# Gates turned in 32x32 blocks on VectorE before they are stored to DRAM, in an attention kernel on one core

## The chip, the core and the metric

The kernel runs on one core of a Trainium2 chip. The metric is the device time of one execution in microseconds (us). Before the change it is 2564.84 us, the median of three runs (2561.96 to 2568.30 us). One more execution was profiled; its trace is what all views below come from.

## The reference, cut to what matters

```python
def _A_ref(x, wqkv, wo):                       # B the same, with its own weights
    B, S, D = x.shape;  H = 32;  Dh = D // H   # S 2048, D 512, Dh 16
    qkv = (x @ wqkv).reshape(B, S, 3, H, Dh).transpose(2, 0, 3, 1, 4)
    q, k, v = qkv[0], qkv[1], qkv[2]
    scores = jnp.einsum("bhqd,bhkd->bhqk", q, k) * (Dh ** -0.5)
    o = jnp.einsum("bhqk,bhkd->bhqd", _softmax(scores), v)
    return o.transpose(0, 2, 1, 3).reshape(B, S, D) @ wo

g = _sigmoid((x * gate_w).sum(-1, keepdims=True))
return g * _A_ref(x, A_wqkv, A_wo) + (1 - g) * _B_ref(x, B_wqkv, B_wo)
```

Two attention blocks of 32 heads each read the same x of 2048 tokens. A gate g per token mixes their outputs. The gate is small: 2048 numbers g and 2048 numbers 1 - g, 16 KB in all.

## The kernel before, in words

**Heads and half heads.** The 64 heads (32 of A, then 32 of B) run one after another through the same pipeline. A head's 2048 queries are taken in two halves. For a half, TensorE multiplies the 16 tiles of 128 keys with the 1024 queries (`score`, L305), ScalarE takes the exponential out of PSUM (L307), and TensorE multiplies the result with v into the accumulator `acc` (L974). Each half ends with a copy of `acc` to a tile `ev` (L997) and its store to the DRAM tensor `od` (L1002).

**The maxima, one half ahead.** The exponential needs the largest score of each query beforehand. TensorE therefore computes the scores of a later half a first time (L234), VectorE takes their maxima (L240, L252), and `max_split` and `max_rows` bring them to the place where the second computation uses them. That trip is made once for each half head, 128 times in all: VectorE turns the tile `mparts` of maxima into `mt` in 32x32 blocks (L270); SP stores `mt` into the DRAM tensor `md` in runs of 32 half-precision numbers, 64 bytes (L273); when that has landed, SP loads two rows of `md` into the rows 48 and 49 of `q_st` (L278, two loads); and the score matmuls of the half contract over 50 rows, these two among them (L305).

**What sets the order.** The order of every engine's instructions is fixed when the program is built. The string `FULL` spells out four rows of 128 queries at a time: letters for score tiles, maxima, products with v and hidden projection pieces. Two lists are emptied along it. `row_ops` holds what has a fixed place: one entry at each letter W or R, with `max_split` and `max_rows` put at its front at every half head. `waiting` holds DMA issues of SP without a fixed place; `drip(1)` pops one of them after every second score tile (L1054). So how many entries stand in `waiting` decides between which other issues of SP each one falls. SP itself works strictly in order: an issue that waits for a semaphore holds up all that stand behind it.

**The gates.** From row 26 + 8*16 on, the gate logits are summed (L560) and `queue_gates` puts nine steps into `row_ops`: eight of arithmetic on [128 x 16] tiles and `spread_gates`. `gate[0]` (g) and `gate[1]` (1 - g) hold token 128*t + p in partition p, column t. `spread_gates` puts 16 DMA issues into `waiting`. The first eight store `gate[s]` into the DRAM tensor `gd[s]`, in the token order that the heads use (issued at L108 through `drip`, and listed under L108 for that reason): each covers 64 partitions and 8 columns, and neighbouring tokens lie in neighbouring partitions, so that no two numbers of one partition are neighbours in DRAM. The other eight load runs of 128 tokens from `gd` into `gate_t` (L580), where all eight heads of a group get a copy. `gate_t` is read at L643, from 681.8 us on; `gate[1]` is read once more at the end (L776).

## Time and profile before

| what | value |
|---|---|
| time, median of 3 runs | 2564.84 us (2561.96 to 2568.30) |
| time of the profiled execution | 2568.01 us |
| its span, first to last instruction | 2566.2 us |
| what lies around the span | 1.8 us |
| mean granted TensorE clock | 0.997 |
| busy: TensorE, VectorE, ScalarE, GpSimd | 98%, 92%, 93%, 17% |
| gate stores (8) issued | 496.7 to 516.6 us |
| gate loads (8) issued | 517.2 to 524.9 us |
| first use of the loaded gates | 681.8 us |

TensorE is nearly never idle: what delays it is lost, since no later slack exists to make up for it. The views name instructions by line, engine, operation and tile: "q_st<-md" is the transfer from `md` into `q_st`. "SPq" stands for the issue of a DMA by SP; its duration is that of the issue, not that of the transfer. "PEld" is TensorE's loading of weights.

### The profile page before, as it was taken

The page shows a single profiled execution, that of the slowest core. Times are in us where ns is not written, and L with a number is a line of the kernel's source. Part 1 is how long each engine was busy: PE and PEld are TensorE (multiplying, and loading weights), DVE is VectorE, ACT ScalarE, POOL GpSimd, SP SyncE. Part 2 cuts the span into 40 slices and gives each one's busy share as a digit, 9 for nine tenths or more (in the row PEclk, how much of TensorE's full clock was granted, in tenths as well). Part 3 has the DMA queues.
Part 4 walks back from the last instruction along what each step waited for, and adds up shares of the span by engine and source line. Part 5 has one row for each costly group of instructions (what it writes and reads, how often), then busy time and mean ns, then how long its engine had stood idle before and what let it go on. Part 6 is the DMA issues. An engine that isn't in the chain of part 4 may idle for free.

```text
span 2566.2 us, 169681 instructions
## 1 busy us (share of the span) xinstructions
PE 2509.2 (98%) x76566; PEld 1608.9 (63%) x76566; DVE 2363.4 (92%) x4587; ACT 2399.0 (93%) x4750; POOL 434.3 (17%) x841
## 2 busy tenths in 40 slices
PE   9999999889999999999999999999999999999997
PEld 4666666556666666666666666655665566665663
DVE  4999999879999999999999999999999999999994
ACT  1899999889999999999999999999999999999995
POOL 3133211211210000111212112112101200002113
PEclk9999999989999999999999999999999999999999
DMA  6533223222211322322222222245113321124103
GB/s 144 149 87 87 69 67 99 51 70 68 79 52 53 84 57 55 102 67 78 70 59 68 68 82 56 67 127 136 41 49 95 90 58 49 36 78 113 46 21 117
DMA packets 150911, 195.24 MB, mean 76 GB/s; under 512 B 45368, under 2 KB 95816, under 8 KB 150184
## 3 DMA queue, kind: packets, MB, share of 16 engines
q1 hardware_dynamic: 144008, 172.45, 24.4%
q8 instruction: 599, 9.81, 1.7%
q0 software_dynamic: 3136, 9.74, 1.4%
q10 hardware_dynamic: 3040, 2.20, 0.3%
q14 instruction: 128, 1.05, 0.1%
HBM read 116.80 MB, written 66.59 MB: 71 GB/s over the span
## 4 chain that ended last, share of the span: by engine, by line
PE 85%; ACT 4%; DVE 4%; DMA 3%; issue 2%; SPq 1%; POOL 1%; ACTq 0%; POOLq 0%; DVEq 0%
PE acc L974 40%; PE ps_m L234 16%; PE ps_st L305 14%; PE ps_p L324 6%; ACT p L307 3%; PE ps_st L234 3%; DVE mxp L240 2%; PE ps_p L705 2%; PE ps_p L346 1%; DVE ev L997 1%; ACT ev L997 1%; PE ps_st L346 1%; DMA q_st<-md 0%; SPq L108 0%; DMA k_st<-early 0%
## 5 line engine op out<-in xcount | busy, mean ns | idle before, releaser
L974 PE MATMUL acc<-p,vg 64*17 64x384 f32 (+1 forms) x34784 | 2186.9, 365 | 18.9 <-issue 7.8
L307 ACT ACTIVATE p<-ps_st 128x512 f32<-128x512 f32 x4068 | 2122.4, 642 | 72.0 <-PE ps_st L305 30.6
L240 DVE TENSOR_REDUCE mxp<-ps_m 128x1 f32<-128x512 f32 x3072 | 1944.2, 683 | 77.8 <-PE ps_m L234 40.4
L305 PE MATMUL ps_st<-q_st,k_st 50*32 50x512 f16 x16272 | 1561.3, 381 | 17.5 <-DMA q_st<-md 13.7
L234 PE MATMUL ps_m<-k_st,q_st 48*32 48x512 f16 x14336 | 1380.3, 377 | 5.5 <-issue 4.0
L974 PEld LDWEIGHTS acc<-p,vg 64*17 64x17 f32 x34784 | 979.8, 93 | 249.0 <-issue 27.2
L305 PEld LDWEIGHTS <-k_st 50*32 50x32 f16 x16384 | 670.5, 90 | 387.8 <-issue 199.6
L234 PEld LDWEIGHTS <-q_st 48*32 48x32 f16 x16384 | 550.3, 90 | 232.6 <-issue 143.3
L324 PE MATMUL ps_p<-x_sb,w 64*32 64x512 f32 x3648 | 477.9, 591 | 0.2 <-issue 0.2
L252 DVE CUSTOM_DVE_ANT_0 rise<-ps_m,rise 128x512 f32<-128x512 f32 x512 | 350.0, 684 | 49.9 <-PE ps_st L305 38.5
L247 ACT ACTIVATE rise<-ps_st 128x512 f32<-128x512 f32 x512 | 316.8, 619 | 35.3 <-PE ps_st L234 23.3
L234 PE MATMUL ps_st<-x_st,q_st 48*32 48x512 f16 x2048 | 225.6, 377 | 1.2 <-DMA x_st<-rise_p 1.2
L264 POOL TENSOR_SCALAR mrow<-mrow 128x8 f32<-128x8 f32 x128 | 29.8, 233 | 1059.9 <-DVE mrow L263 1059.4
L371 POOL CAST parts<-stage 128x512 f16<-128x512 f32 x56 | 34.1, 610 | 809.0 <-ACT stage L832 438.1
L705 PE MATMUL ps_p<-w_big,ot 64*32 64x512 f32 x1024 | 134.4, 591 | 0.0
L324 PE MATMUL ps_p<-w_big,x_sb 64*32 64x512 f32 x1024 | 133.8, 590 | 0.0
L324 PEld LDWEIGHTS ps_p<-x_sb,w 64*32 64x32 f32 x3648 | 116.5, 106 | 18.7 <-issue 5.1
L705 PE MATMUL ps_p<-wo_b,ot 64*32 64x512 f32 x768 | 100.6, 591 | 1.9 <-ACT added L917 1.5
L346 PE MATMUL ps_p<-w_big,x_sb 64*32 64x256 f32 x1280 | 86.4, 376 | 0.0
L372 POOL TENSOR_TENSOR parts<-stage,parts 128x512 f16<-128x512 f32 x56 | 65.3, 1165 | 4.5
L346 PEld LDWEIGHTS ps_p<-w_big,x_sb 64*32 64x32 f32 x1280 | 42.2, 106 | 13.0 <-issue 1.4
L997 DVE COPY ev<-acc 128x512 f32<-128x512 f32 x64 | 44.2, 690 | 1.2 <-PE ps_p L324 0.4
(115 smaller groups left out, 836.2 us busy)
## 6 DMA issues: line engine op xcount, KB each, us to landing
od<-ev SPq DMA_DIRECT2D x126, 256.0 KB
k_st<-kd SPq DMA_DIRECT2D x126, 128.0 KB
q_st<-qd SPq DMA_DIRECT2D x126, 128.0 KB
vd<-v_st SPq DMA_DIRECT2D x64, 136.0 KB
vg<-vd POOLq DMA_DIRECT2D x32, 272.0 KB, 4.0
k_st<-kd SPq DMA_DIRECT2D x126, 64.0 KB
q_st<-qd SPq DMA_DIRECT2D x126, 64.0 KB
kd<-parts SPq DMA_DIRECT2D x56, 128.0 KB
```

The lines of the kernel that those rows point to most:

```text
L234: pe.matmul(ps[j:j + 32], q[b:b + SC, t * P + j:t * P + j + 32], k[b:b + SC], start=True, stop=True, tile_position=(b, j))
L240: dve.tensor_reduce(o[:, c:c + 1], ps, op=ALU.max, axis=AX.X)
L247: act.activation(rises[m], ps, AF.Relu)
L252: dve.tensor_tensor_reduce(out=rise, in0=ps, in1=rise, scale=1.0, scalar=LOWEST, op0=ALU.add, op1=ALU.max, accum_out=o[:, 0:1])
L305: pe.matmul(ps[j:j + 32], k[b:b + SC + 2, kk * P + j:kk * P + j + 32], qv(b), start=True, stop=True, tile_position=(b, j))
L307: act.activation(pt[u][:, c * 512:(c + 1) * 512], ps, AF.Exp, scale=SCALE / UNIT ** 2)
L324: pe.matmul(ps[j:j + 32], a, m, start=k == 0, stop=k == last, tile_position=(b, j))
L346: pe.matmul(ps[j:j + 32, e * 256:(e + 1) * 256], x_sb[b:b + 64, i, k, o:o + 32], w_big[b:b + 64, k, g * P:(g + 2) * P], start=k == e == 0, ...
L372: pool.tensor_tensor(t[:n, 1], v[:n], t[:n, 0], op=ALU.subtract)
L705: pe.matmul(ps[j:j + 32], T["o"][b:b + 64, k, o + j % 64:o + j % 64 + 32], w[b:b + 64, g], start=first, stop=last, tile_position=(b, j))
L974: pe.matmul(acc[d:d + 17, qa * P:qb * P], v[b:b + 64, 2 * (w % n) + c if h == NH - 1 else w % n, j], pt[u][b:b + 64, c * 512 + qa * P:c * ...
L997: (dve.tensor_copy if w < NT or h == NH - 2 else act.copy)(ev, acc)
```

## The change

The two gate tiles become the two halves of one tile [128 x 2 x 16], and the two DRAM tensors one tensor [2, 2048]. VectorE turns the [128 x 32] tile in 32x32 blocks into a new tile `gate_r`: there a partition 32*a + 16*s + t holds the 32 tokens 128*t + 32*a to 128*t + 32*a + 31, so that one partition's 32 numbers are 128 neighbouring bytes in DRAM. Four stores, one for each a, take the place of eight. The eight loads into `gate_t` read the same order of tokens as before.

```diff
-    gd = [dram.tile([S], F32, name=f"gd{s}") for s in range(2)]
+    gd = dram.tile([2, S], F32, name="gd")
...
-    gate = [core.tile([P, NT], F32, name=f"gate{i}") for i in range(2)]
+    gates = core.tile([P, 2, NT], F32, name="gate")
+    gate = [gates[:, i] for i in range(2)]
...
     def spread_gates():
+        turned = core.tile([P, 32], F32, name="gate_r")
+        dve.transpose(turned, gates.rearrange("p s t -> p (s t)"))
+
+        def store_part(a):
+            nc.sync.dma_start(bass.AP(tensor=gd.tensor, offset=gd.offset + a // 2 * 512 + a % 2 * 32,
+                                      ap=[[1024, 4], [64, NT // 2], [1, 32]]), turned[32 * a:32 * a + 32])
+
         def one(s, i, f):
-            o = gd[s]
             nc.sync.dma_start(gate_t[s][f * 64 + i * 32:f * 64 + i * 32 + 32], bass.AP(
-                tensor=o.tensor, offset=o.offset + i * 1024 + f * 512, ap=[[0, HG], [P, 4], [1, P]]))
-
-        for s in range(2):
-            o = gd[s]
-            for i in range(2):
-                for f in range(2):
-                    waiting.append((nc.sync.dma_start, bass.AP(
-                        tensor=o.tensor, offset=o.offset + i * 1024 + f * 512, ap=[[1, 64], [64, NT // 2]]),
-                        gate[s][f * 64:f * 64 + 64, i * NT // 2:(i + 1) * NT // 2]))
+                tensor=gd.tensor, offset=gd.offset + s * S + i * 1024 + f * 512, ap=[[0, HG], [P, 4], [1, P]]))
+
+        waiting.extend((store_part, a) for a in range(4))
         waiting.extend((one, s, i, f) for s in range(2) for i in range(2) for f in range(2))
```

Four entries fewer in `waiting` move the issues of SP against each other. This is SP's order before, from the last projection store ahead of the gates; `kd`, `xd` and `qd` take projections, and `w` is the next group's weights:

```order
L366 DMA xd_97<-rise_p 64x2x512
L108 DMA gd_116<-gate_1604 64x8x1 x4
L108 DMA gd_117<-gate_1605 64x8x1 x2
L273 DMA md_115<-mt 4x32x32
L278 DMA q_st_231<-md_115 2x1024 x2
L108 DMA gd_117<-gate_1605 64x8x1 x2
L580 DMA gate_t_1611<-gd_116 32x1x128 x4
L580 DMA gate_t_1612<-gd_117 32x1x128 x4
L1002 DMA od_106<-ev 128x512
L360 DMA qd_81<-parts 64x2x512 x2
L118 DMA w_15244<-in_wqkv_a 64x4x128 x4
```

Six gate stores stand ahead of the store of the maxima (`md`), and no gate load. The same place now, each row with the semaphores that it waits for (DMAHW0 to DMAHW7 count the transfers of SP in turn; each transfer takes the next one):

```order
L366 DMA xd_97<-rise_p 64x2x512 [waits DMAHW4_49,Pool_49]
L583 DMA gd<-gate_r 4x8x32 [waits DMAHW5_49]
L583 DMA gd<-gate_r 4x8x32 [waits DMAHW6_49]
L583 DMA gd<-gate_r 4x8x32 [waits DMAHW7_49]
L583 DMA gd<-gate_r 4x8x32 [waits DMAHW0_49]
L587 DMA gate_t_1609<-gd 32x1x128 [waits DMAHW6_49,DMAHW5_49,DMAHW1_49]
L587 DMA gate_t_1609<-gd 32x1x128 [waits DMAHW7_49,DMAHW2_49,DMAHW0_49]
L273 DMA md_115<-mt 4x32x32 [waits DMAHW3_49,DVE_49]
L278 DMA q_st_230<-md_115 2x1024 [waits DMAHW4_49,DMAHW3_49]
L278 DMA q_st_230<-md_115 2x1024
L587 DMA gate_t_1609<-gd 32x1x128 x2
L118 DMA w_15085<-in_wqkv_a 64x4x128 [waits DMAHW4_49,PE_49]
```

All four gate stores and the first two gate loads now stand ahead of the store of the maxima, and these two loads wait for the gate stores (DMAHW5, 6, 7 and 0). The weight load has moved ahead of the store of `ev`. On VectorE one row is added, behind the two gate steps and half a head ahead of those stores:

```order
L240 TENSOR_REDUCE mxp<-ps_m 128x1 x2
L572 TENSOR_TENSOR gate<-gate_u,gate_e 128x16
L1072 TENSOR_SCALAR gate<-gate 128x16
L580 STREAM_TRANSPOSE gate_r<-gate 128x32
L252 ISA rise,mxp<-ps_m,rise 128x512
```

Here L580 is a line of the changed kernel: the blockwise turn of the gates. The orders of TensorE, ScalarE and GpSimd are the same as before.

## Prediction

> **What bounds the kernel now.** I read the page first, for the engine that sets the time; then stretches of the trace cut at equal places of the program, for where it loses; then the waits, SP's own timeline and VectorE's in the worst stretch.

> ```profile
> PE 2509.2 (98%) x76566; PEld 1608.9 (63%) x76566; DVE 2363.4 (92%) x4587; ACT 2399.0 (93%) x4750; POOL 434.3 (17%) x841
> PE   9999999889999999999999999999999999999997
> PEclk9999999989999999999999999999999999999999
> ```

> TensorE is busy 98% of the span. In 40 slices of 64 us only the eighth and ninth (449 to 577 us) fall under nine tenths before the end, and in the ninth the granted clock falls too. The gate stores are issued in just these slices. The turn of the maxima (L270) comes once in each half head, so stretches from one turn to the next hold equal work:

> ```profile
> core 0: us, PE busy (x) PEld busy (x) DVE busy (x) ACT busy (x) POOL busy (x), PEclk, DMA share, GB/s
> 478.97:498.28 19.31, 19.17 (x600) 12.89 (x602) 18.55 (x39) 18.87 (x38) 5.41 (x8) 1.00 0.28 71
> 498.28:537.59 39.31, 23.09 (x600) 13.53 (x602) 18.72 (x37) 19.47 (x38) 2.47 (x6) 0.83 0.17 30
> 537.59:556.53 18.94, 18.89 (x600) 12.56 (x602) 18.27 (x37) 18.66 (x38) 3.23 (x6) 1.00 0.37 102
> 556.53:575.46 18.93, 18.85 (x600) 12.61 (x601) 18.23 (x36) 18.65 (x38) 3.96 (x8) 1.00 0.27 74
> ```

> Each has 600 matmuls. One takes 39.31 us where the next two take 18.94 and 18.93: 20.4 us are lost. TensorE's idle time there is 39.31 - 23.09 = 16.2 us against 0.1 in the next ones; the other 4.2 us (23.09 against 18.89) are matmuls at a lower granted clock, 0.83 on the mean. What ends the idle time:

> ```profile
> PE ps_st L305 <- DMA q_st<-md: 11.5, 1, 11.5
> 503.98 0.41 PE L234 MATMUL ps_m<-k_st,q_st 48*32 48x512 f16 x3 [1.59 <-issue]
> 509.61 0.45 PE L974 MATMUL acc<-p,vg 64*17 64x256 f32 x3 [2.76 <-issue]
> ```

> The longest wait, 11.5 us, is for the rows of maxima. Two more, 1.6 and 2.8 us, have no releaser in the trace; they fall into the same time. SP shows why the maxima are late:

> ```profile
> 496.06 0.57 SPq L366 DMA_DIRECT2D xd<-rise_p  x1
> 496.69 9.00 SPq L108 DMA_DIRECT2D gd<-gate  x6
> 505.78 1.46 SPq L273 DMA_DIRECT2D md<-mt  x1
> 515.35 0.53 SPq L278 DMA_DIRECT2D q_st<-md  x2
> 515.93 1.27 SPq L108 DMA_DIRECT2D gd<-gate  x2
> 517.24 8.25 SPq L580 DMA_DIRECT2D gate_t<-gd  x8
> ...
> 479.20 0.58 SPq L273 DMA_DIRECT2D md<-mt  x1
> 481.18 0.53 SPq L278 DMA_DIRECT2D q_st<-md  x2
> ```

> The last two rows are the same trip one half head earlier. There `md` is issued 0.23 us after the turn, and its landing lets the load go 481.18 - 479.20 = 1.98 us after that. In the bad stretch the six gate stores hold SP for 9.0 us, so that `md` goes 505.78 - 498.28 = 7.5 us after the turn; it then takes 9.57 us (to 515.35), and TensorE starts again only at 522.74, 11.53 us after it stopped at 511.21. The traffic of the time is small in bytes and large in number:

> ```profile
> DMA packets 4201, 0.22 MB, mean 10 GB/s; under 512 B 4058, under 2 KB 4194, under 8 KB 4198
> gd<-gate SPq DMA_DIRECT2D x8, 2.0 KB
> md<-mt SPq DMA_DIRECT2D x1, 8.0 KB
> 522.74 0.62 PE L305 MATMUL ps_st<-q_st,k_st 50*32 50x512 f16 x4 [11.53 <-DMA q_st<-md]
> ```

> The first row is for 496.5 to 518 us: 4201 packets for 0.22 MB. A gate store of 2 KB in runs of 4 bytes is 512 pieces, the eight are 4096; `md` is 8 KB in 128 runs of 64 bytes. So I read the loss as one cause, 4096 single-element writes, with three effects: SP held, the maxima's two transfers slow, and other waits of TensorE in the same time.

> **The change part by part.**

> *The single elements go.* 4096 pieces of 4 bytes become 4 x 32 = 128 runs of 128 bytes, the count that `md` has in every half head, where it costs 1.98 us to its landing and no idle time of note. If the stretch falls to the length of its neighbours, the gain is 39.31 - 18.94 = 20.4 us; against the stretch before it (19.31, with the gate arithmetic on GpSimd and VectorE in it) it is 20.0 us. I take -20.4 us, then subtract what the new order costs.

> *The turn on VectorE.* It comes behind the two last gate steps:

> ```profile
> 478.97 0.20 DVE L270 STREAM_TRANSPOSE mt<-mparts 128x32 f16<-128x32 f16 x1
> 480.58 0.17 DVE L1071 TENSOR_SCALAR gate<-gate 128x16 f32<-128x16 f32 x1
> 480.86 0.69 DVE L252 CUSTOM_DVE_ANT_0 rise<-ps_m,rise 128x512 f32<-128x512 f32 x1
> 498.28 0.20 DVE L270 STREAM_TRANSPOSE mt<-mparts 128x32 f16<-128x32 f16 x1
> ```

> The nearest row is the turn of `mparts`, the same 128x32 at half the bytes: 0.20 us. With 32-bit numbers I bound it by 0.2 and 0.4 us and take 0.2. It delays the maximum at 480.86. VectorE is busy 18.55 of 19.31 us in that stretch, so 0.76 us of slack stand against it: 0 to 0.4 us, taken as 0.1. Its result is ready 16 us before the first store needs it.

> *The wait that stands ahead of the maxima now.* SP issues four stores and two gate loads before `md`, and the second load waits until the last two stores have landed. Queued behind that wait are `md`, the two `q_st` loads that TensorE needs, six more gate loads, the weight load and the store of `ev`. The clock of it: SP is free at 496.69, after `xd`. Below are, in this order, two gate stores of the chain of waits before SP was held (issue 0.63 us, a step of 0.68 from one to the next), SP's timeline in two other half heads, TensorE's wait in the first of these, and both as stretches from turn to turn:

> ```profile
> 499.54 0.63 SPq L108
> 500.22 0.64 SPq L108
> ...
> 1658.95 3.90 SPq L140 DMA_DIRECT2D wo_b<-in_wo_b  x5
> 1662.94 0.58 SPq L273 DMA_DIRECT2D md<-mt  x1
> 1665.32 0.99 SPq L278 DMA_DIRECT2D q_st<-md  x2
> 1280.71 0.58 SPq L273 DMA_DIRECT2D md<-mt  x1
> 1283.02 0.53 SPq L278 DMA_DIRECT2D q_st<-md  x2
> PE ps_st L305 <- DMA q_st<-md: 1.7, 1, 1.7
> 1278.47:1297.45 18.98, 18.90 (x600) 12.41 (x602) 18.25 (x37) 18.74 (x38) 2.46 (x6) 1.00 0.27 76
> 1659.47:1679.16 19.69, 17.61 (x508) 9.15 (x501) 18.07 (x40) 18.32 (x39) 1.14 (x5) 1.00 0.57 162
> ```

> The fourth store is issued at 496.69 + 3 x 0.68 = 498.7 and has landed, priced like `md`, 1.98 us later at 500.7. The first load has gone before that; the second goes at 500.7 and takes 0.65 to 1.03 us (8.25 / 8). So `md` goes at about 501.4 instead of 498.5, the `q_st` loads at 503.4 to 503.8 (1.98 to 2.38 us, the latter from 1662.94 to 1665.32, where other issues are close by), and SP has issued both by 504.3 at the latest: 5.6 to 6.0 us after the turn at 498.28. How late is too late, these two half heads tell, where loads of weights stood ahead of the maxima. With the loads issued by 1283.02 + 0.53, 5.1 us after the turn at 1278.47, the half head takes 18.98 us: nothing lost. With 1665.32 + 0.99, 6.8 us after the turn at 1659.47 (five loads of `wo_b` stood ahead), TensorE waits 1.7 us and the half head takes 19.69, 0.75 us more than 18.94. Between these, 5.6 to 6.0 us cost 0.2 to 0.4 us. A landing of 3.6 us in place of 2, because gate loads run beside it, would make it 1 to 2 us. I take 0.5 us, with 0 and 2 as ends. The granted clock in the row of 1659.47 is 1.00, so a wait of this size doesn't slow the matmuls behind it.

> *What else moves.* The weight load now comes before the store of `ev`. Its tile was last read for the projections whose results `xd` stores at 496.06, so I cost it at nothing; were the tile still in use, the store of `ev` would wait behind it, and two `ev` buffers cover that for one half head. `gate_t` is used at 681.8 us: at nothing.

> The sum: -20.4 + 0.5 + 0.1 = -19.8 us. Against the profiled execution that is 2568.01 - 19.8 = 2548.2 us (its span 2566.2 - 19.8 = 2546.4, with the same 1.8 us around it). The profiled execution stands 3.2 us above the median; taking the same difference off the median gives 2564.84 - 19.8 = **2545.0 us**.

> **The rivals.**

> *A wait takes the place of the one removed (10%).* The 128-byte stores might land as late as `md` did in the bad stretch, 9.57 us after issue instead of 1.98. Then the second gate load goes at 498.7 + 9.57 = 508.3, `md` at 508.9, the `q_st` loads are issued by 511.5, 13.2 us after the turn. That is 6.4 us beyond the case of 1659.47, where TensorE waited 1.7, so it waits 8.1 us; with the loss to the clock in the proportion of the bad stretch (20.4 lost for 16.2 idle), 10.2 us. Gain 10.2, time 2554.6. Against it: `md` itself has runs half as long, as many of them, and lands in 1.98 us. [...]

> *Slower: the stores still go out by single elements (3%).* Should a partition's 32 numbers be cut into 4-byte pieces, four stores of 1024 pieces stand ahead of the maxima in place of six of 512, and SP also waits for their landing. At 9.00 / 6 = 1.5 us for 512 pieces they hold SP 12 us, to 508.7; the last lands 9.57 us after its issue at 505.7, at 515.3; gate load, `md` and its landing (2 to 9.6 us) and the loads end at 519 to 526, and with the 6.9 us that followed in the bad stretch (515.88 to 522.74) TensorE starts at 526 to 533 instead of 522.74. That is 3 to 10 us slower: 2568 to 2575. It decides as soon as the stores need over some 20 us from first issue to landing. Against it: the run is contiguous on both sides, in a partition of `gate_r` and in DRAM.

> *No gain: without the profiler the stall isn't there (4%).* Then the times of the unprofiled runs would lack it already, and the change moves nothing: 2564.8. Against it: unprofiled runs would have to be 20 us under the profiled one; the median is 3.2 under, the fastest (2561.96) 6.1. This bounds what the stall costs without the profiler to 14 us at the least, and is why I let the range reach up.

> **How the numbers follow.** The forecast has 83%, with a range of its own of 2542 to 2552: 2545.0, down by the 0.6 us of added cost and the spread of the runs (2.9 below the median), up by 2 us for the wait and 5 for a smaller stall outside the profile. The first rival has 10%, no gain 4%, slower 3%. What a measurement of this kernel can tell from no change is some 0.3%, 7.7 us. Forecast and first rival both lie beyond that; of the forecast's weight I move 1% to "same" for a smaller stall. So faster 0.92, same 0.06 (no gain, that 1%, and the part of the slower case under 7.7 us), slower 0.02. A range of 2541 to 2556 takes in the forecast and the first rival and leaves out under a tenth by the cases; my unknown is the size outside the profile.

> **What would show it.** Right: the stretch of 39.31 us becomes one of 19 to 20 with 600 matmuls at a granted clock of 1.00; the four gate stores take about 2.7 us of SP; `md` follows the turn by about 3 us and its landing takes about 2; the wait for the maxima is under 2 us; packets under 512 bytes fall by some 3970 of the 45368 of the page. The unnamed waits of 1.6 and 2.8 us have to vanish too: if they stay, they had another cause. Wrong: `md` landing after 5 us or more (first rival), gate stores holding SP for several us each (slower), or a new long wait elsewhere that takes the 20 us back.

## The result, and the profile after

| | before | changed |
|---|---|---|
| time, median | 2563.40 us (4 runs, 2560.11 to 2568.30) | 2545.81 us (4 runs, 2545.46 to 2549.03) |
| ratio | | 0.9933, 95% interval 0.9914 to 0.9951 |
| profiled execution, its span | 2568.01, 2566.2 us | 2545.46, 2543.7 us |
| half head in which the gates are stored | 39.31 us | 19.03 us |

The change makes the kernel faster by 0.67% (0.49% to 0.86%), 17.2 us of 2563.4. The forecast was 2545.0 us. The kernel before has one more run here than ahead of the prediction, hence 2563.40 in place of 2564.84. The profiled execution of the changed kernel is one of its four runs.

The first lines of the page of the changed kernel are the busy time of each engine, then TensorE and its granted clock in 40 slices, then the DMA packets of the whole span:

```profile
PE 2503.8 (98%) x76566; PEld 1610.5 (63%) x76566; DVE 2363.4 (93%) x4588; ACT 2396.5 (94%) x4750; POOL 433.4 (17%) x841
PE   8999999999999999999999999999999999999997
PEclk9999999999999999999999999999999999999999
DMA packets 146831, 195.24 MB, mean 77 GB/s; under 512 B 41288, under 2 KB 91736, under 8 KB 146104
```

The dent in the eighth and ninth slices is gone, and with it the dip of the clock. Packets under 512 bytes fell from 45368 to 41288, by 4080 where some 3970 were forecast; the new stores account for 3968 (4096 less 128), what the other 112 were, no view shows. The stretches from one turn of the maxima to the next, with the gate stores in the middle one, as before (span, then busy time of each engine, granted clock, DMA share, GB/s):

```profile
480.15:499.15 19.00, 18.89 (x599) 12.51 (x601) 18.62 (x39) 18.72 (x38) 5.39 (x8) 1.00 0.29 73
499.15:518.18 19.03, 18.95 (x602) 12.51 (x607) 18.24 (x36) 18.69 (x38) 2.46 (x6) 1.00 0.28 82
518.18:537.07 18.89, 18.84 (x599) 12.52 (x597) 18.22 (x37) 18.64 (x37) 3.22 (x6) 1.00 0.30 81
```

39.31 us became 19.03, as good as its neighbours. SP's timeline in the changed kernel around the gates:

```profile
496.93 0.57 SPq L366 DMA_DIRECT2D xd<-rise_p  x1
497.55 2.60 SPq L583 DMA_DIRECT2D gd<-gate_r  x4
500.27 1.70 SPq L587 DMA_DIRECT2D gate_t<-gd  x2
502.06 0.57 SPq L273 DMA_DIRECT2D md<-mt  x1
504.04 0.53 SPq L278 DMA_DIRECT2D q_st<-md  x2
```

Four stores take 2.60 us, the two gate loads with their wait 1.70, and the maxima go at 502.06, 2.91 us after their turn; 1.98 us later they have landed and are loaded. What TensorE still waits for them, among the waits of 499 to 519 us, and the two turns on VectorE:

```profile
PEld L305 <- DMA q_st<-md: 0.4, 1, 0.4
```

```profile
481.97 0.21 DVE L580 STREAM_TRANSPOSE gate_r<-gate 128x32 f32<-128x32 f32 x1
499.15 0.20 DVE L270 STREAM_TRANSPOSE mt<-mparts 128x32 f16<-128x32 f16 x1
```

The profiled executions differ by 22.5 us, 20.3 of them in this stretch. The rest lies where the change does nothing: the half head that took 21.23 us at 1789.8 in the trace before takes 18.93 in the trace after, and a start that is 2.4 us longer after (64.29 against 61.91 us to the first turn) is made up in other places. Differences of this kind stand between other traces too: the half head right ahead of the one with the gate stores takes 18.94 to 19.31 us in the thirteen traces of this case.

### The profile page after: what moved, and what is told of

It reads as the page before. It is cut to its first block, busy times and chain, and to the rows that moved or that the text cites. A ratio compares the mean times of both kernels' runs of the same rounds, so it can differ in the third digit from the quotient of the medians.

```text
span 2543.7 us, 169678 instructions
## 1 busy us (share of the span) xinstructions
PE 2503.8 (98%) x76566; PEld 1610.5 (63%) x76566; DVE 2363.4 (93%) x4588; ACT 2396.5 (94%) x4750; POOL 433.4 (17%) x841
## 2 busy tenths in 40 slices
DMA packets 146831, 195.24 MB, mean 77 GB/s; under 512 B 41288, under 2 KB 91736, under 8 KB 146104
## 4 chain that ended last, share of the span: by engine, by line
PE 85%; ACT 5%; DVE 4%; DMA 2%; issue 2%; SPq 0%; POOL 0%; ACTq 0%; POOLq 0%; DVEq 0%
PE acc L975 40%; PE ps_m L234 16%; PE ps_st L305 14%; PE ps_p L324 6%; ACT p L307 3%; PE ps_st L234 3%; DVE mxp L240 3%; PE ps_p L706 2%; PE ps_p L346 1%; DVE ev L998 1%; ACT ev L998 1%; PE ps_st L346 1%; DMA md<-mt 0%; PE ps_m L324 0%; DMA w<-in_wqkv_a 0%
## 5 line engine op out<-in xcount | busy, mean ns | idle before, releaser
L305 PE MATMUL ps_st<-q_st,k_st 50*32 50x512 f16 x16272 | 1558.4, 380 | 7.4 <-ACT p L307 2.4
L234 PE MATMUL ps_m<-k_st,q_st 48*32 48x512 f16 x14336 | 1377.2, 377 | 3.5 <-issue 2.7
L305 PEld LDWEIGHTS <-k_st 50*32 50x32 f16 x16384 | 671.5, 90 | 381.5 <-issue 200.1
L234 PEld LDWEIGHTS <-q_st 48*32 48x32 f16 x16384 | 549.3, 90 | 232.0 <-issue 141.7
L252 DVE CUSTOM_DVE_ANT_0 rise<-ps_m,rise 128x512 f32<-128x512 f32 x512 | 349.6, 683 | 49.9 <-PE ps_st L305 39.1
L234 PE MATMUL ps_st<-x_st,q_st 48*32 48x512 f16 x2048 | 224.9, 377 | 0.0
```

The source lines that it names most:

```text
L234: pe.matmul(ps[j:j + 32], q[b:b + SC, t * P + j:t * P + j + 32], k[b:b + SC], start=True, stop=True, tile_position=(b, j))
L252: dve.tensor_tensor_reduce(out=rise, in0=ps, in1=rise, scale=1.0, scalar=LOWEST, op0=ALU.add, op1=ALU.max, accum_out=o[:, 0:1])
L305: pe.matmul(ps[j:j + 32], k[b:b + SC + 2, kk * P + j:kk * P + j + 32], qv(b), start=True, stop=True, tile_position=(b, j))
```

## The experiments

The time came out as forecast; what was open was why 4096 single elements cost 20 us. The prediction had it that their number did, with SP held, the maxima late and TensorE waiting in other places as the effects. Rivals: that a piece under some length is slow for itself; that pieces disturb each other where they lie close together in memory; and that something else in the change, such as the place of the weight load, brought the gain.

Most runs are the changed kernel with eight more stores into a DRAM tensor `dump` that nothing reads. They are put into the waiting list ahead of the new gate stores, so that six of them fall into the places of the six old ones, ahead of the store of the maxima. They differ in the length of a piece and in where the pieces lie. The measure is the half head from turn to turn, 19.03 us without them, and the time from the issue of `md` to that of the load behind it, 1.98 us without them. The ratios are to the kernel before, run again beside these runs (2565.79 us, median of 13); they are not exactly the quotients of the medians. The numbers under "How close is too close" are of one profiled execution each; the half head ahead of the one compared differs by up to 0.4 us from one execution to another (18.94 to 19.31 us, as above), another one by 2.3 (21.23 against 18.93 us above).

### Single elements put back beside the new stores

```diff
+    dump = dram.tile([2, S], F32, name="dump")
+    pad = core.tile([P, 8, 1], F32, name="pad")
+    pool.memset(pad, 0.0)
...
+        def store_extra(s, i, f):
+            nc.sync.dma_start(bass.AP(tensor=dump.tensor, offset=dump.offset + (s * S + i * 1024 + f * 512) * 1,
+                                      ap=[[1, 64], [64, NT // 2]]), pad[f * 64:f * 64 + 64][:, :, 0])
+
+        waiting.extend((store_extra, n // 4, n // 2 % 2, n % 2) for n in range(8))
         waiting.extend((store_part, a) for a in range(4))
```

> The changed kernel with eight more stores of 64 x 8 single numbers of 4 bytes into a scratch tensor of DRAM, in the places of SP's order where the old gate stores stood (six ahead of the store of the maxima, two behind); the gates go as in the change. If the single-element stores alone cost what the old kernel lost, the half head comes back to 38 to 40 us from turn to turn and the time to that of the kernel before (2560 to 2568 us). If the cause was anything else that the change touched (the dependency on two tensors, the place of the weight load), the half head stays at 19 to 20 us.

Measured: 2571.0 us median of 8, 1.0017 of the kernel before (1.0003 to 1.0031), a little over the 2560 to 2568 us expected. The stretch, and SP's timeline in it:

```profile
497.93:538.18 40.25, 24.11 (x600) 13.56 (x601) 18.72 (x36) 19.41 (x38) 2.46 (x6) 0.79 0.14 20
```

```profile
496.35 9.01 SPq L594 DMA_DIRECT2D dump<-pad  x6
505.46 0.56 SPq L274 DMA_DIRECT2D md<-mt  x1
515.42 0.53 SPq L279 DMA_DIRECT2D q_st<-md  x2
```

The old picture is back to within a microsecond: six stores hold SP for 9.01 us (9.00 before), `md` takes 9.96 us (9.57), the half head 40.25 (39.31). The single elements alone account for the whole loss of the stretch; nothing else in the change is needed to explain the gain.

### The same elements, 256 bytes apart

```diff
-    dump = dram.tile([2, S], F32, name="dump")
+    dump = dram.tile([2, S, 64], F32, name="dump")
...
-                                      ap=[[1, 64], [64, NT // 2]]), pad[f * 64:f * 64 + 64][:, :, 0])
+                                      ap=[[64, 64], [64 * 64, NT // 2]]), pad[f * 64:f * 64 + 64][:, :, 0])
```

(The offset is scaled by 64 too.)

> As the run extra4, but each of the 4096 numbers lies 256 bytes from the next in DRAM, so that no two share a block of 256 bytes. If the number of pieces sets the cost: 38 to 40 us again. If the cost comes from neighbouring pieces being written into the same short block of memory by different queues at the same time: 19 to 25 us.

Measured: 2549.1 us, median of 2, ratio 0.9927 (0.9899 to 0.9956).

```profile
496.47:516.59 20.12, 19.03 (x600) 12.59 (x602) 18.33 (x37) 18.77 (x38) 2.46 (x6) 1.00 0.24 39
```

```profile
494.87 5.19 SPq L594 DMA_DIRECT2D dump<-pad  x6
500.16 0.56 SPq L274 DMA_DIRECT2D md<-mt  x1
502.47 0.53 SPq L279 DMA_DIRECT2D q_st<-md  x2
```

As many pieces of as few bytes cost 1.1 us instead of 21. `md` lands in 2.31 us. SP is still held for 5.19 us. So neither the number of pieces nor their length is the cause by itself: in these runs where they lie decides.

### As many pieces of 64 bytes

```diff
-    dump = dram.tile([2, S], F32, name="dump")
-    pad = core.tile([P, 8, 1], F32, name="pad")
+    dump = dram.tile([2, S, 16], F32, name="dump")
+    pad = core.tile([P, 8, 16], F32, name="pad")
...
-                                      ap=[[1, 64], [64, NT // 2]]), pad[f * 64:f * 64 + 64][:, :, 0])
+                                      ap=[[16, 64], [16 * 64, NT // 2], [1, 16]]), pad[f * 64:f * 64 + 64])
```

(The offset is scaled by 16 too.)

> As the run extra4 with the same 4096 pieces, but of 64 bytes each (256 KB in all, neighbours in DRAM adjacent). If the number of pieces sets the cost: 38 to 40 us. If the length of a piece does, and 64 bytes are long enough, as the stores of the maxima have them: SP is still held by the issues for some us, and the half head takes 19 to 30 us. [...]

Measured: 2548.5 us, median of 3, ratio 0.9934 (0.9906 to 0.9962).

```profile
496.81:515.94 19.13, 19.03 (x601) 12.51 (x602) 18.24 (x37) 18.70 (x38) 2.46 (x6) 1.00 0.27 53
```

4096 pieces, adjacent, with 16 times the bytes, cost 0.1 us and leave the landing of `md` at 2.01 us. How fast such pieces are themselves was not measured.

### How close is too close

Three runs move the single elements 64, 32 and 16 bytes apart (a step of 16, 8 and 4 numbers in place of 64 in the access pattern). One keeps eight neighbours together, but takes them from one partition, with the partitions 256 bytes apart:

```diff
-                                      ap=[[1, 64], [64, NT // 2]]), pad[f * 64:f * 64 + 64][:, :, 0])
+                                      ap=[[64, 64], [1, NT // 2]]), pad[f * 64:f * 64 + 64, :, 0])
```

(For this `dump` is [2, S, 8], `pad` is [P, 8, 2] and the offset is scaled by 8.)

Two lengthen adjacent pieces to 16 and 32 bytes (`dump` [2, S, 4] and [2, S, 8]). One halves the number of adjacent elements (`range(4)`); there four extra stores and two of the new gate stores stand ahead of the store of the maxima.

> As the run extra4, the 4096 numbers 64 bytes apart in DRAM. If two pieces disturb each other only within 64 bytes or less: the half head stays at 19 to 21 us, as with 256 bytes between them (20.1). If the block in which they disturb each other is 256 bytes, four pieces share one, and the half head takes 22 to 40 us.

> As the run extra4, the numbers 32 bytes apart, so that two share 64 bytes. If the block is 64 bytes: some loss, 21 to 40 us; if it is 32 bytes or less: 19 to 21 us.

> 4096 numbers of 4 bytes again, eight neighbours at a time in 32 bytes of DRAM, but the eight come from one partition and the partitions lie 256 bytes apart. [...] If sharing the block is enough, whoever writes: a loss that is smaller than with 64 to a block, 22 to 40 us.

> As the run extra4 with half the extra stores (2048 numbers, adjacent), and two of the new gate stores behind them, all ahead of the store of the maxima. If the loss grows with the number of adjacent pieces: about half of extra4's 21 us, a half head of 27 to 32 us. If the loss is that of a deadline missed by the same event each time: 35 us or more; if a slack hides the first half: 19 to 23 us.

> As the run extra4, the 4096 numbers 16 bytes apart, two to each 32 bytes of DRAM. With one number to 32 bytes the half head took 20.4 us, with eight neighbours in 32 bytes 30.3, with numbers adjacent throughout 40.3. If what costs is two writes into the same 32 bytes: 22 to 30 us. If the length of the chain of writes into one block is what counts (eight or more): 20 to 22 us.

> The 4096 pieces with 16 bytes each, adjacent, two to each 32 bytes. If sharing a block of 32 bytes costs whatever the length: the same as extra4_s16, 22 to 30 us. If only pieces as short as 4 bytes do: 19 to 20 us, as with 64 bytes.

> The 4096 pieces with 32 bytes each, adjacent. If the block is 32 bytes, each piece fills its own: 19 to 20 us. If it is 64 bytes, two share one: the same as extra16.

The stretches from turn to turn, first 64, 32 and 16 bytes apart, then eight from one partition and half the number, then pieces of 16 and of 32 bytes; each row is of its own kernel. The times of these seven executions (2548.7 to 2556.4 us) do not follow the stretches: 2548.7 us has the one of 23.13, 2556.4 the one of 20.43. The rest of an execution varies by as much, so the stretches are what is compared.

```profile
499.11:519.07 19.96, 19.07 (x601) 12.45 (x606) 18.33 (x37) 18.79 (x38) 2.46 (x6) 1.00 0.24 38
```

```profile
500.84:521.27 20.43, 19.10 (x603) 12.46 (x607) 18.33 (x37) 18.79 (x38) 2.46 (x6) 1.00 0.24 37
```

```profile
496.72:519.85 23.13, 21.05 (x600) 12.94 (x602) 18.56 (x37) 18.97 (x38) 2.47 (x6) 1.00 0.21 34
```

```profile
494.07:524.37 30.30, 21.41 (x600) 12.99 (x602) 18.62 (x37) 19.20 (x38) 2.47 (x6) 0.89 0.16 26
```

```profile
499.32:525.86 26.54, 21.85 (x605) 13.19 (x611) 18.54 (x37) 19.11 (x38) 2.46 (x6) 1.00 0.20 44
```

```profile
497.86:523.06 25.20, 21.28 (x600) 13.06 (x601) 18.52 (x36) 19.25 (x38) 2.47 (x6) 0.93 0.19 33
```

```profile
499.06:519.77 20.71, 19.02 (x600) 12.50 (x601) 18.32 (x36) 18.75 (x38) 2.46 (x6) 1.00 0.23 43
```

In one table, ordered by how many pieces share 32 bytes of DRAM. The landing is the time from the issue of `md` to the issue of the load that waits for it, from SP's timeline of each run; the loss is the half head less 19.03 us. These are SP's rows for 32 bytes apart, then for 16 bytes apart:

```profile
504.18 0.56 SPq L274 DMA_DIRECT2D md<-mt  x1
507.21 0.53 SPq L279 DMA_DIRECT2D q_st<-md  x2
```

```profile
499.86 0.56 SPq L274 DMA_DIRECT2D md<-mt  x1
505.72 0.53 SPq L279 DMA_DIRECT2D q_st<-md  x2
```

All runs together:

| pieces (4096 where nothing else is said) | in 32 bytes | half head | loss | landing of `md` |
|---|---|---|---|---|
| 64 bytes, adjacent | 1 | 19.13 us | 0.1 | 2.01 us |
| 4 bytes, 64 bytes apart | 1 | 19.96 | 0.9 | 2.89 |
| 4 bytes, 256 bytes apart | 1 | 20.12 | 1.1 | 2.31 |
| 4 bytes, 32 bytes apart | 1 | 20.43 | 1.4 | 3.03 |
| 32 bytes, adjacent | 1 | 20.71 | 1.7 | 1.96 |
| 4 bytes, 16 bytes apart | 2 | 23.13 | 4.1 | 5.86 |
| 16 bytes, adjacent | 2 | 25.20 | 6.2 | 5.89 |
| 4 bytes, adjacent, 2048 of them | 8 | 26.54 | 7.5 | 8.63 |
| 4 bytes, eight from one partition | 8 | 30.30 | 11.3 | 9.85 |
| 4 bytes, adjacent | 8 | 40.25 | 21.2 | 9.96 |

The step lies between one piece and two in 32 bytes: the landing of `md` goes from 2 to 3 us to 5.9, at 4 bytes and at 16 alike. That the eight come from one partition doesn't spare them, so pieces from different partitions are not needed for it. Nor is it the length of DRAM that the pieces are spread over: eight from one partition and elements 32 bytes apart both cover 128 KB, and lose 11.3 and 1.4 us. The number counts too, once they share: 2048 lose 7.5 us where 4096 lose 21.2. Two half heads fell outside what was expected: 26.54 us with half the number (27 to 32), 20.71 with 32-byte pieces (19 to 20). The losses of 0.9 to 1.7 us with one piece in 32 bytes fit a deadline: the six stores hold SP for 4.5 to 6.3 us ahead of the maxima, and TensorE waits 0.8, 1.0, 1.2 and 1.6 us for `q_st` (in the table's order). SP in the run with pieces of 32 bytes:

```profile
497.45 6.29 SPq L594 DMA_DIRECT2D dump<-pad  x6
503.84 0.56 SPq L274 DMA_DIRECT2D md<-mt  x1
505.80 0.53 SPq L279 DMA_DIRECT2D q_st<-md  x2
```

Here the landing is as quick as ever (1.96 us), but the loads of the maxima are issued only by 506.33, 7.3 us after the turn at 499.06, and TensorE waits 1.6 us for them.

The same count for the other runs tells how far the late maxima go as an explanation. From the turn to the end of the issue of both loads it takes 5.4 us in the changed kernel, 5.5 with 64-byte pieces, then 6.5 (64 and 256 bytes apart), 6.9 (32 bytes apart) and 7.3, and with shared blocks 9.5 (16 bytes apart), 10.4 (16-byte pieces), 13.0 (half the number), 14.4 (eight from one partition) and 18.0 (all adjacent). Less 5.5 us, that is the loss to within 0.1 us in all rows up to 13.0 but one (16-byte pieces lose 1.2 us more). The two heaviest lose 2.4 and 8.7 us on top, and the kernel before (17.6 us after the turn) 8.2: there the late maxima do not account for the whole. This is an agreement of times; no run delays the loads alone.
### The old stores, behind the maxima

The kernel before, with its eight stores issued right behind the loads of the maxima instead of ahead of them (from 502.02 us on in place of 496.69), and the gate loads some half heads after them:

```diff
+    gates_done = []
...
-            (spread_gates,)))
+            (gates_done.append, 1)))
...
+        early_stores = []
...
-                    waiting.append((nc.sync.dma_start, bass.AP(
+                    early_stores.append((nc.sync.dma_start, bass.AP(
...
-        waiting.extend((one, s, i, f) for s in range(2) for i in range(2) for f in range(2))
+        waiting[0:0] = early_stores
+        at(now[0] // 2 * 2 + 32, lambda: waiting.extend((one, s, i, f) for s in range(2) for i in range(2) for f in range(2)))
...
             row_ops[0:0] = [(max_split, h, f // 8), (None,), (max_rows, h, f // 8)]
+            if gates_done:
+                row_ops.insert(3, (spread_gates,))
+                gates_done.clear()
```

> The kernel before, with its eight single-element gate stores put directly behind the loads of the maxima of the next half head, and the eight gate loads two and a half half heads later. The next trip of the maxima is due 16 us after the first of these stores. If the loss came from the order alone (SP held ahead of the maxima), the half head in which the stores run stays at 19 to 20 us and the time is that of the changed kernel (2545 to 2549 us). If the writes themselves slow everything for their 20 to 25 us, the waits of TensorE without a releaser (1.6 and 2.8 us in the kernel before) stay, and the next trip of the maxima is late as well: two half heads lose 5 to 20 us between them.

(The gate loads came at 591 us, more than four half heads after the stores, not two and a half as this says.)

Measured: 2559.8 us, median of 5, ratio 0.9981 (0.9954 to 1.0008), which is not told from no change. SP, the two half heads, and TensorE's long waits in the first:

```profile
499.09 0.58 SPq L273 DMA_DIRECT2D md<-mt  x1
501.44 0.53 SPq L278 DMA_DIRECT2D q_st<-md  x2
502.02 11.38 SPq L108 DMA_DIRECT2D gd<-gate  x8
```

```profile
497.37:530.91 33.54, 26.10 (x599) 15.45 (x600) 18.80 (x36) 19.82 (x38) 2.44 (x6) 0.85 0.38 42
530.91:549.86 18.95, 18.90 (x600) 12.58 (x601) 18.27 (x37) 18.67 (x38) 3.22 (x6) 1.00 0.30 81
```

```profile
511.56 1.07 PE L978 MATMUL acc<-p,vg 64*17 64x512 f32 x3 [3.55 <-issue]
524.00 0.42 PE L978 MATMUL acc<-p,vg 64*17 64x128 f32 x2 [2.74 <-issue]
```

No maxima are late here: their loads are issued ahead of the stores, and the wait for them is not among the waits of the stretch. Still the half head takes 33.54 us, 14.5 more than 19.03. TensorE stands idle for 7.4 us of it (33.54 - 26.10), with waits of 3.55 and 2.74 us for nothing that the trace shows. Two pieces of the stretch, the first inside the longer wait, the second behind it:

```profile
509.00:511.00 2.00, 0.00 (x0) 0.00 (x0) 0.00 (x0) 0.00 (x0) 0.00 (x0) 0.82 0.01 0
513.00:515.00 2.00, 2.00 (x35) 1.16 (x26) 0.90 (x2) 1.44 (x3) 0.00 (x0) 0.50 0.27 2
```

In the first no engine works, and the DMA engines hardly do (a busy share of 0.01). In the second the granted clock is 0.50. TensorE is busy for its 599 matmuls 7.2 us longer than the 18.9 of the next half head, in part at this lower clock: 35 matmuls in the 2.00 us at 0.50, where the next half head has 601 in 18.95 us at 1.00.

So moving the stores behind the maxima saves 5.8 us of the stretch (39.31 - 33.54) and leaves 14.5: a loss of that size needs no late maxima. How the 20.3 us of the kernel before divide, this run doesn't say: there one wait can hide another, and here all eight stores go in one burst, with four weight loads ahead of `md` where six gate stores stood. The other part of the expectation, that the next trip suffers too, did not come: the next half head takes 18.95 us.

## Why the prediction was right, and where its reason was not

**Size and place of the gain: right.** The stretch was to lose 20.4 us and to pay 0.6 for the new order, 19.8 in all; it measured 39.31 - 19.03 = 20.3, with the costs in it. The time was 2545.81 us against 2545.0.

**The wait ahead of the maxima: right.** `md` was put at 501.4, 3.1 us after the turn at 498.28, behind four stores and two loads; it went 2.91 us after. The stores took 2.60 us of SP (2.7), the landing 1.98 (1.98 to 2.38; the 3.6 us of its bad case, which the trace before shows at 88.65, did not come). The cost of 0.5 us shows as a wait of 0.4 us in TensorE's weight load; against the half head behind it the stretch is 0.14 us longer, so that it came out nearer to 0.1. The bound from two other half heads served well: the loads were issued 5.4 us after the turn, where 5.1 cost nothing and 6.8 cost 0.75.

**The turn on VectorE: right.** 0.21 us against 0.20; VectorE's half head of 19.00 us shows no cost.

**From the profiled execution to the median: right by luck.** The prediction took the profiled execution's 3.2 us above the median as something that stays. After the change the profiled execution is 0.35 us under the median. The gain between medians is 17.6 us and between profiled executions 22.5; the sum of 19.8 lies between them, and the distance of a single profiled execution from the median is chance in size.

**The cause: wrong.** The step that failed is the one from "small in bytes and large in number" to "one cause, 4096 single-element writes". The row at 481.18 shows 128 pieces of 64 bytes landed in 1.98 us. It cannot tell which of the three ways in which they differ from the gate stores (number, length, place) matters, and I read it as the number. 4096 pieces of 64 bytes cost 0.1 us and 4096 of 4 bytes, 256 bytes apart, 1.1. What costs in these runs is that several pieces share 32 bytes of DRAM: `md` beside single elements lands in 3.03 us with one in 32 bytes, in 5.86 with two. The sum came out right all the same, because it took the whole loss from the trace and because the new stores differ from the old in all three ways: as far as the cause goes, that was luck.

**"Three effects": right in kind, their shares open.** With one piece in 32 bytes, 4.50 us of SP's being held (64-byte pieces, the loads issued 5.5 us after the turn) lose 0.1 us, 5.19 us (256 bytes apart, 6.5 us after it) 1.1, and 6.29 us (32-byte pieces, 7.3 us after it) 1.7. Waits without a releaser need no late maxima: with the maxima on time there are two of 3.55 and 2.74 us (1.59 and 2.76 before). As forecast, they vanished with the change.

**"The other 4.2 us are matmuls at a lower granted clock": too simple.** TensorE is busy 21.05 us with the elements 16 bytes apart and 21.85 with half the number, 2.0 to 2.9 us more than 18.95 to 19.03 at a granted clock of 1.00 throughout. So busy time grows here without a lower clock too; how the 4.2 us divide is not shown.

**The rivals.** A wait in place of the one removed: `md` landed in 1.98 us, not 9.57. Stores that still go out by single elements: no, 128 pieces. No gain without the profiler: the medians of four runs each differ by 17.6 us.

## What to carry to other kernels

Look where neighbouring single elements go, not only at how many there are: here stores whose pieces share 32 bytes of DRAM went with a landing of 9.57 us in place of 1.98 for a transfer that has nothing to do with them, and with 20.3 us of the half head, at 16 KB of data. Turning the tile first so that a partition's numbers are neighbours in DRAM cost 0.21 us of VectorE; here 32-byte pieces (1.7 us lost) or single elements 32 bytes apart (1.4 us) already left little of the loss of 21.2. The adjacent single elements showed in the profile by issues of 1.5 us each (9.01 us for six, against 5.19 with the elements 256 bytes apart) and by a stretch with many packets, few bytes (4201 for 0.22 MB from 496.5 to 518 us before), and waits for other transfers or for nothing.

## What the runs showed of the hardware that was not expected

```profile
507.00:509.00 2.00, 1.92 (x34) 0.73 (x33) 1.30 (x3) 1.09 (x2) 0.00 (x0) 1.00 0.00 0
509.00:511.00 2.00, 1.55 (x26) 0.89 (x27) 1.20 (x2) 0.60 (x1) 0.00 (x0) 1.00 0.00 0
```

So the trace shows no packets at work that `md` would have to wait behind in these 4 us. Where the time goes is open.

- **Engines wait while such writes run.** In the last experiment the maxima are not late, and 14.5 us are lost, half as idle time of TensorE (7.4 us, 7.2 of them without a releaser), half as longer busy time (7.2 us), in part at a granted clock of 0.50. What the engines wait for is open. One thing that slows in the same time is the loading of instructions. The queue of instructions from 496.5 to 518 us (packets, MB, share of 16 engines' time), first of the kernel before, then of the changed one:

```profile
q8 instruction: 3, 0.05, 2.4%
```

```profile
q8 instruction: 5, 0.08, 1.6%
```

A packet takes 2.4% x 16 x 21.5 / 3 = 2.8 us before and 1.6% x 16 x 21.5 / 5 = 1.1 us after. Whether that is the cause of the waits was not tried: no run changes the instructions' loading alone.
